# Branch products in pieces of 512 columns: two token blocks against one weight pair

## Chip, cores and metric

The kernel runs on one core of one Trainium2 chip. The metric is the device time of a launch in microseconds: 1518.65 us, the median of three runs (1518.39 to 1519.7).

## What is computed

```python
def _moe2_ref(x, w1, w2, w3, w_out):
    h = np.maximum(np.maximum(x @ w1, x @ w2), x @ w3)
    return (h @ w_out).astype(np.float32)

def reference(**kwargs):
    attn_out = _attn_ref(**attn_kwargs)          # retention, 8 x 8 heads, 576 positions, width 64
    x = attn_out.transpose(0, 2, 1, 3).reshape(4608, 512)
    x = _moe_ref(x=x, **moe_kwargs)              # h = x @ w_in (2048 wide); (h * cos(h)) @ w_out
    return _moe2_ref(x=x, **moe2_kwargs)         # three branches of 512 x 768, their maximum, 768 x 512
```

The change touches the three branch products `x @ w1`, `x @ w2`, `x @ w3` and their maximum, and nothing else of the arithmetic.

## The kernel before

The 4608 tokens are cut into nine blocks of 512 (`NBLK`). The stages follow one another on TensorE: retention with the first half of `w_in`, the second half of `w_in`, `w_out` (tiles `wo`), the three branches (tiles `d_b`, `b_b`, `a_b`), the last product (tiles `o`). Each big matrix product is a Strassen-like scheme: a weight pair (two column tiles of 128 features, four quarters) and a token block in four quarters of 256 columns give seven products, `P_A11` to `P_S4`. Weights and tokens are split into a high and a low part in a reduced fp32 form, so that one product with one pair is six matmuls: low weight by high token and high by high for two halves of the contraction, then high by low twice (`product_in`, L373).

There are nine branch pairs, b0 to b8 (`PAIRS`). All nine stand in SBUF through the branch stage: eight in the eight buffers of `wpool`, b8 in four tiles of `xpool`. `xpool` has 22 buffers of 4 KB a partition, for operands and for results. For every block, `group_in` (L405) takes one or two pairs (`B_GROUPS`: two pairs side by side fill the 512 columns of a PSUM bank, 256 each) and runs the seven products in a fixed order, one per slot. A slot is a call of `tick()`, which runs what was entered in the agenda with `at(n, fn)` for that slot: so the code writes out by hand the order of every engine's instructions. The last product of a group, `P_A22`, is put off to the fifth slot of the next group (`pending`, `last_product`). ScalarE copies three results out of PSUM at L400, L418, L423 and L430, VectorE adds three more at L410, and the maxima run on VectorE at L901 from `branch_half`. A block's seven operands (`build_in`, L661) need four differences, seven copies to the high part on ScalarE (L360) and seven subtractions for the low part on VectorE (L364), 512 columns each; they are made during the block before. The maxima are stored to DRAM tiles `mq` and read back in the last stage by `build_out`. SyncE's queue issues every DMA in the order of the code.

Of the kernel before, what the change touches and what calls it, by code (L numbers as in the profile page):

```python
# [101 lines left out]
def retention_ffn(ctx: ExitStack, tc: tile.TileContext, att, w_in, w_out, w123, w_out2, cst, out):  # L102
# [34 lines left out]
    def at(n, fn):  # L137
        agenda.setdefault(slot[0] + n, []).append(fn)
# [175 lines left out]
        at(6 + more, lambda: st["lows"]())  # L314

    def take(kind, i):
        if (kind, i) == ("b", 8):
            ws = []
            for k in range(4):
                lo, hi = PIECE[k]  # L320
                t = x4(f"w_{kind}{i}_{k}", [hi - lo, 2, HB], F32R)
                nc.sync.dma_start(out=f32(t), in_=stash[kind, i][:, lo:hi])
                ws += [t[:, n] for n in range(hi - lo)]
            weights[kind, i] = ws
            return
# [40 lines left out]
    def load_quarters(o, src):  # L366
        n = o["n"]
        for k in range(2):
            t = o[f"k{k + 1}"] = x4(f"k{k}_{o['name']}", [2, n])
            nc.sync.dma_start(out=t, in_=src[:, 2 * k : 2 * k + 2])  # L370


    def product_in(h, ws, product, x, first):  # L373
        for p, w in enumerate(ws):
# [9 lines left out]
            for i, (a, b) in enumerate(terms):  # L384
# [6 lines left out]
                    skip_group_check=True,  # L391
                )

    pending = []

    def last_product(own_slot=True):

        g = pending.pop()
        product_in(g["d"], g["ws"], P_A22, g["xs"], False)
# [5 lines left out]
    def group_in(ws, xs, name, done, where):  # L405
        n = HB * len(ws)
        g = {"ws": ws, "xs": xs, "name": name, "n": n, "done": done, "at": where}

        def plus(dst, b):
            nc.vector.tensor_tensor(out=dst, in0=dst, in1=b[:, :n], op=ALU.add)  # L410

        def go(b, product, first):
            product_in(b, ws, product, xs, first)

        d = g["d"] = bank(f"d_{name}")
        go(d, P_A11, True)
        s0 = g["s0"] = x4(f"s0_{name}", [2, n])
# [4 lines left out]
        s1 = g["s1"] = x4(f"s1_{name}", [2, n])  # L422
# [454 lines left out]
        )  # L877
    for i in range(len(back) - 3):
        at(28 * i + 5, lambda: background(*back.pop(0), False))
    for k in range(4):  # L880
        for p in range(2):
            at(28 * (NBLK - 1) + 7 * k + 8 + p, lambda k=k, p=p: take("b", 2 * k + p))
    later_y = {}

    def block_in(j, now, k1, k2):
        o = later_y[j] = {"name": f"z{j}", "n": NB}
        at(now, lambda: load_quarters(o, x2q[j]))
# [9 lines left out]
    def store(dst, s):  # L897
        nc.sync.dma_start(out=dst, in_=s)

    def most(dst, a, b):  # L900
        nc.vector.tensor_tensor(out=dst, in0=a, in1=b, op=ALU.max)  # L901

    def branch_half(g, half):
        j, k = g["at"]
        if k in (0, 1) and half:
            best[j, k] = g["s0"]
            at(1, lambda: most(g["s0"], g["s0"], g["s1"]))
        elif k == 2:
            s = g[f"s{half}"]
            at(1, lambda: most(s, s, best.pop((j, half))))  # L910
            at(3, lambda: store(mq[j][0][:, 2 * half : 2 * half + 2], s))
        elif k == 3 and half:
            best[j, k] = g
        elif k == 4 and half:

            def both():
                o = best.pop((j, 3))
                most(g["s0"], g["s0"], g["s1"])
                for p in range(2):
                    s = o[f"s{p}"]  # L920
                    most(s, s, g["s0"][:, :, p * HB : (p + 1) * HB])
                    at(2, lambda p=p, s=s: store(mq[j][1][:, 2 * p : 2 * p + 2], s))

            at(1, both)

    B_GROUPS = [[0, 1], [2, 3], [4, 5], [6], [7, 8]]
    for j in range(NBLK):
        for k, ids in enumerate(B_GROUPS):
            if k == 0 and 1 <= j <= 3:
                background(*back.pop(0), False)  # L930
            if k == 2 and j + 1 < NBLK:
                block_in(j + 1, 4, 9, 13)
            if j == NBLK - 1 and k in (1, 2):
                at(6, lambda k=k: [take("o", i) for i in ((0, 1), (2,))[k - 1]])
            if j == NBLK - 1 and k == 4:
                outs[0, 0] = build_out("m0_0", NB, mq[0][0], range(1, 7), -0)
            group_in([weights["b", i] for i in ids], later_y[j], f"b{j}_{k}", branch_half, (j, k))

    todo = [(j, k) for j in range(NBLK) for k in range(2)]
    outs[0, 1] = build_out("m0_1", HB, mq[0][1], (0, 0, 1, 1, 2, 2), 0)  # L940
    for j in range(1, NBLK):
        at(14 * j - 14, lambda j=j: outs.__setitem__((j, 0), build_out(f"m{j}_0", NB, mq[j][0], (4, 5, 6, 8, 10, 12), 0)))
        at(14 * j - 8, lambda j=j: outs.__setitem__((j, 1), build_out(f"m{j}_1", HB, mq[j][1], (8, 8, 9, 9, 10, 10), 2)))
# [50 lines left out]
```

## Time and profile before

| | us |
|---|---|
| median of three runs | 1518.65 |
| the profiled execution, first to last instruction | 1516.2 |
| the branch stage in it, first to last branch matmul | 958.5 to 1378.6 |
| PE busy, whole span | 1454.9 (96%) |
| PEld (weight loads) busy | 1416.0 (93%) |
| DVE busy | 1224.6 (81%) |
| ACT busy | 726.8 (48%) |
| POOL busy | 268.7 (18%) |

The page shows busy shares by engine; PE is TensorE's matmuls, PEld its weight loads, which run beside the matmuls, DVE is VectorE, ACT ScalarE, POOL GpSimd, SP SyncE. Matmuls overlap in their records, so the number of matmuls that start in a stretch tells more than the length of one. Idle time before an instruction is put down to what ended it (the releaser).

### The profile page before, as it was taken

The page shows a single profiled execution, that of the slowest core. Times are in us where ns is not written, and L with a number is a line of the kernel's source. Part 1 is how long each engine was busy: PE and PEld are TensorE (multiplying, and loading weights), DVE is VectorE, ACT ScalarE, POOL GpSimd, SP SyncE. Part 2 cuts the span into 40 slices and gives each one's busy share as a digit, 9 for nine tenths or more (in the row PEclk, how much of TensorE's full clock was granted, in tenths as well). Part 3 has the DMA queues.
Part 4 walks back from the last instruction along what each step waited for, and adds up shares of the span by engine and source line. Part 5 has one row for each costly group of instructions (what it writes and reads, how often), then busy time and mean ns, then how long its engine had stood idle before and what let it go on. Part 6 is the DMA issues. An engine that isn't in the chain of part 4 may idle for free.

```text
span 1516.2 us, 30767 instructions
## 1 busy us (share of the span) xinstructions
PE 1454.9 (96%) x12506; PEld 1416.0 (93%) x12506; DVE 1224.6 (81%) x1759; ACT 726.8 (48%) x1214; POOL 268.7 (18%) x216
## 2 busy tenths in 40 slices
PE   6899999999899997899999999999999999999998
PEld 5798989998889997899999999999999999999998
DVE  6888999989889989999999998656664555538997
ACT  3555555556667755454445444334432333323332
POOL 3344444444222001100000000000000000004221
PEclk9899999999999998999999999999999999999999
DMA  7588888876989984556555568923431110254443
GB/s 292 181 292 304 309 300 301 318 290 240 355 304 364 328 294 156 184 193 215 193 203 195 196 216 323 397 107 119 147 127 48 70 66 34 70 191 163 168 168 138
DMA packets 83084, 324.46 MB, mean 214 GB/s; under 512 B 9216, under 2 KB 9216, under 8 KB 76928
## 3 DMA queue, kind: packets, MB, share of 16 engines
q1 hardware_dynamic: 82944, 322.51, 59.4%
q8 instruction: 98, 1.61, 0.4%
q14 instruction: 42, 0.34, 0.1%
HBM read 190.35 MB, written 132.12 MB: 213 GB/s over the span
## 4 chain that ended last, share of the span: by engine, by line
PE 46%; DVE 6%; issue 3%; DMA 2%; ACT 1%; POOL 0%; DVEq 0%; SPq 0%; ACTq 0%; POOLq 0%
PE wo L795 17%; PE d_b L385 14%; PE b_b L385 7%; PE o L795 4%; PE a_b L385 3%; DVE l_m L768 1%; DMA st_o<-p_o 1%; DVE tb_m L356 1%; DVE o_o L808 1%; DVE x_m L759 1%; DVE u_o L808 1%; DMA raw_b<-w 1%; DVE l_g L768 0%; DMA k_m<-mq 0%; ACT h_m L763 0%
## 5 line engine op out<-in xcount | busy, mean ns | idle before, releaser
L795 PE MATMUL wo<-h_g,w_wo 128*128 128x256 f32 x1728 | 314.9, 284 | 0.0
L795 PEld LDWEIGHTS wo<-h_g,w_wo 128*128 128x128 f32 x1728 | 271.3, 193 | 0.0
L795 PE MATMUL wo<-l_g,w_wo 128*128 128x256 f32 x864 | 246.6, 285 | 7.6 <-DVE l_g L768 7.6
L385 PE MATMUL d_b<-x_z,w_b 128*128 128x256 f32 x1944 | 248.8, 283 | 2.9 <-ACT s_b L430 2.1
L385 PEld LDWEIGHTS d_b<-x_z,w_b 128*128 128x128 f32 x1944 | 239.9, 192 | 3.7 <-ACT s_b L430 2.7
L795 PEld LDWEIGHTS wo<-l_g,w_wo 128*128 128x128 f32 x864 | 166.7, 193 | 9.6 <-DVE l_g L768 9.5
L385 PE MATMUL b_b<-x_z,w_b 128*128 128x256 f32 x972 | 131.6, 283 | 2.0 <-DVE x_z L364 2.0
L385 PE MATMUL d_a<-x_x,w_wi 128*128 128x256 f32 x864 | 123.2, 293 | 4.1 <-DVE x_x L364 2.9
L385 PEld LDWEIGHTS b_b<-x_z,w_b 128*128 128x128 f32 x972 | 123.2, 192 | 2.2 <-DVE x_z L364 2.2
L385 PE MATMUL d_a<-x_y,w_wi 128*128 128x256 f32 x864 | 115.3, 291 | 9.2 <-ACT s_a L418 5.8
L385 PEld LDWEIGHTS d_a<-x_y,w_wi 128*128 128x128 f32 x864 | 110.9, 199 | 10.4 <-ACT s_a L418 6.5
L385 PEld LDWEIGHTS d_a<-x_x,w_wi 128*128 128x128 f32 x864 | 110.2, 195 | 8.9 <-DVE x_x L364 4.1
L795 PE MATMUL o<-h_m,w_o 128*128 128x256 f32 x648 | 117.5, 283 | 0.0
L763 ACT CAST h_g<-tb_g 128x1024 fp32r<-128x1024 f32 x36 | 37.8, 1051 | 150.5 <-DVE tb_g L356 145.9
L795 PEld LDWEIGHTS o<-h_m,w_o 128*128 128x128 f32 x648 | 101.1, 192 | 0.0
L452 DVE SCALAR_TENSOR_TENSOR t_a<-s_a,t_a 128x1024 f32<-128x1024 f32 x72 | 99.8, 1389 | 1.4 <-ACT t_a L448 1.4
L410 DVE TENSOR_TENSOR s_b<-s_b,b_b 128x512 f32<-128x512 f32 (+1 forms) x45 | 28.5, 634 | 87.1 <-PE b_b L385 87.0
L460 DVE TENSOR_TENSOR s_a<-s_a,t_a 128x1024 f32<-128x1024 f32 x72 | 90.6, 1274 | 5.9 <-ACT t_a L457 5.9
L457 ACT ACTIVATE t_a<-t_a 128x1024 f32<-128x1024 f32 x72 | 76.3, 1062 | 34.8 <-DVE t_a L453 25.6
L410 DVE TENSOR_TENSOR s_b<-s_b,a_b 128x512 f32<-128x512 f32 (+1 forms) x45 | 28.5, 634 | 79.2 <-PE a_b L385 69.4
L795 PE MATMUL o<-l_m,w_o 128*128 128x256 f32 x324 | 91.8, 283 | 0.0
L418 ACT COPY s_b<-d_b 128x512 f32<-128x512 f32 (+1 forms) x45 | 24.5, 544 | 127.3 <-PE d_b L385 120.0
(173 smaller groups left out, 3003.1 us busy)
## 6 DMA issues: line engine op xcount, KB each, us to landing
u<-att SPq DMA_DIRECT2D x36, 1024.0 KB, 7.3
gq<-s_a SPq DMA_DIRECT2D x72, 512.0 KB, 6.4
k_g<-gq SPq DMA_DIRECT2D x72, 512.0 KB, 6.6
xs<-x_x SPq DMA_DIRECT2D x63, 512.0 KB, 7.3
x_y<-xs SPq DMA_DIRECT2D x63, 512.0 KB, 7.9
w_b<-st_b SPq DMA_DIRECT2D x8, 1792.0 KB, 13.0
st_b<-p_b SPq DMA_DIRECT2D x27, 512.0 KB, 3.8
raw_b<-w SPq DMA_DIRECT2D x18, 512.0 KB, 6.1
```

Of the source, the lines that this page charges most:

```text
L356: eng.tensor_tensor(out=d, in0=a, in1=b, op=ALU.subtract)
L385: nc.tensor.matmul(h[:, p * HB : (p + 1) * HB], a, b, start=first and p == 0 and i == 0, stop=i == len(terms) - 1, skip_group_check=True,)
L410: nc.vector.tensor_tensor(out=dst, in0=dst, in1=b[:, :n], op=ALU.add)
L418: nc.scalar.copy(s0[:, 0], d[:, :n])
L452: nc.vector.scalar_tensor_tensor(out=r, in0=s, scalar=INV2PI, in1=st["t"], op0=ALU.mult, op1=ALU.subtract)
L457: nc.scalar.activation(r, r, AF.Sin, scale=TURN, bias=HALF_PI)
L460: nc.vector.tensor_tensor(out=s, in0=s, in1=f32(st["t"]), op=ALU.mult)
L759: nc.vector.tensor_tensor(out=o["x"][:, 1], in0=o["k1"][:, 0], in1=f32(o["x"][:, 0]), op=ALU.subtract)
L763: nc.scalar.copy(h, o[pairs[k][2]])
L768: nc.vector.tensor_tensor(out=lo, in0=o[pairs[k][2]], in1=f32(h), op=ALU.subtract)
L795: nc.tensor.matmul(b[:, mt * HB : (mt + 1) * HB], a, v, start=first and mt == 0 and p == 0 and i == 0, stop=last and p == len(ws) - 1 and ...
L808: nc.vector.scalar_tensor_tensor(out=d, in0=b, scalar=scale, in1=other, op0=ALU.mult, op1=ALU.add)
```

## The change

One block (block 0) stays alone; the other eight make four duos of two blocks (`NDUO`). For a duo, `product_duo` multiplies one weight pair with both blocks: the moving operand is [128, 2 blocks, 256] columns, 512 in one matmul, and fills a PSUM bank. Six matmuls of 512 columns stand where twelve of 256 stood. The nine pairs come in three turns of three groups, one pair in each group: turns 0 and 1 (pairs b0, b2, b4 and b1, b3, b5) run for duo 0, 1, 2, 3; then the pairs b7, b8, b6 are loaded in the place of b0, b2, b4, and turn 2 runs for duo 3, 2, 1, 0. So six pairs stand in SBUF at a time, and the operands of duos 0 to 2 are built twice, those of block 0 too. Two buffers of `wpool` become six places for results (`held`, `give`). `duo_in` writes out the operand build of a duo slot by slot: four loads of 512 KB from `x2p`, four differences, seven high and seven low parts, 1024 elements a partition each; new operands take the buffers of old ones as TensorE leaves them. Both tiles of DRAM (`x2p`, `mqp`) hold two blocks side by side, so that the stores to them go in pieces of 2 KB and 1 KB a partition. The last stage takes the blocks in the order 7, 8, 5, 6, 3, 4, 1, 2, 0.

```diff
+    def product_duo(h, w, product, x, first):
+        wh, wl = w[product][:, 0], w[product][:, 1]
+        xh, xl = x[product]
+        terms = []
+        for kc in range(2):
+            m = slice(kc * 128, kc * 128 + 128)
+            terms += [(wl[:, m], xh[:, :, kc]), (wh[:, m], xh[:, :, kc])]
+        for kc in range(2):
+            m = slice(kc * 128, kc * 128 + 128)
+            terms.append((wh[:, m], xl[:, :, kc]))
+        dst = h.rearrange("p (b n) -> p b n", b=2)
+        for i, (a, b) in enumerate(terms):
+            nc.tensor.matmul(
+                dst, a, b, start=first and i == 0, stop=i == len(terms) - 1, skip_group_check=True
+            )
...
-    for k in range(4):
+    for k in range(3):
         for p in range(2):
             at(28 * (NBLK - 1) + 7 * k + 8 + p, lambda k=k, p=p: take("b", 2 * k + p))
...
-    take("b", 8)
+    free = []
+    for n in range(2):
+        w = w14(f"ext{n}", F32)
+        free += [w[:, 2 * NB * i : 2 * NB * (i + 1)] for i in range(3)]
...
+    def duo_half(g, half):
+        m, turn, k = g["at"]
...
+            def keep():
+                src = s.rearrange("p q (b n) -> p q b n", b=2)
+                for b in range(2):
+                    nc.sync.dma_start(out=to[:, b], in_=src[:, :, b])
+                give(f"s{half}_{name}")
+
+            at(1, finish)
+            at(3, keep)
...
+        steps = (
+            (-14, load, 0),
+            (-13, load, 1),
+            (-13, load, 3),
+            (-12, load, 2),
+            (-8, less, 4, 1, 0),
+            (-7, high, P_A11, 0),
+            (-6, less, 6, 3, 4),
+            (-6, low, P_A11),
+            (-4, less, 5, 3, 1),
+            (-3, high, P_S1, 4),
+            (0, low, P_S1),
+            (1, high, P_A12, 2),
+            (1, less, 7, 6, 2),
...
+            (6, low, P_A22),
+        )
+        for n, fn, *args in steps:
+            at(to + n, lambda fn=fn, args=args: fn(*args))
...
+    DUO_GROUPS = [(0, 2, 4), (1, 3, 5), (7, 8, 6)]
...
+    duo_in(0, "e0", 16)
+    for k in range(3):
+        single_group(k)
+    for m in range(NDUO):
+        if m < 3:
+            at(1, lambda: background(*back.pop(0), False))
+        duo_groups(m, 0)
+        if m + 1 < NDUO:
+            duo_in(m + 1, f"e{m + 1}", 14)
+        else:
+            for n, i in enumerate((7, 8, 6)):
+                at(7 * n - 7 if n else 0, lambda i=i: take("b", i))
+        duo_groups(m, 1)
+    for n, m in enumerate(reversed(range(NDUO))):
...
+            if k == 0:
+                if m:
+                    duo_in(m - 1, f"e{m - 1}b", 14)
+                else:
+                    block_in(0, 2, 10, 13)
+
+        duo_groups(m, 2, begin)
...
+    for k in (3, 4):
...
+        single_group(k)
```

On TensorE, a group before: block 1 with the pairs b2 and b3 (`d`, `b`, `a` are the group's three PSUM banks, `x_z1_…` the operands of block 1).

```order
L385 MATMUL d_b1_1_11698<-x_z1_0_11439,w_b2_10876 128x256 x6
L385 MATMUL d_b1_1_11698<-x_z1_0_11439,w_b3_10894 128x256 x6
L385 MATMUL b_b1_1_11715<-x_z1_3_11462,w_b2_10876 128x256 x6
L385 MATMUL b_b1_1_11715<-x_z1_3_11462,w_b3_10894 128x256 x6
L385 MATMUL a_b1_1_11730<-x_z1_1_11482,w_b2_10876 128x256 x6
L385 MATMUL a_b1_1_11730<-x_z1_1_11482,w_b3_10894 128x256 x6
```

The same three products in the changed kernel: duo 0 with the pair b3 (`h0_e0` and `l0_e0` are the high and low part of the duo's first operand).

```order
L402 MATMUL d_e0_3_11689<-h0_e0_11252,w_b3_10882 128x512 x4
L402 MATMUL d_e0_3_11689<-l0_e0_11269,w_b3_10882 128x512 x2
L402 MATMUL b_e0_3_11701<-h3_e0_11314,w_b3_10882 128x512 x4
L402 MATMUL b_e0_3_11701<-l3_e0_11357,w_b3_10882 128x512 x2
L402 MATMUL a_e0_3_11713<-h1_e0_11372,w_b3_10882 128x512 x4
L402 MATMUL a_e0_3_11713<-l1_e0_11389,w_b3_10882 128x512 x2
```

Each slot has half the matmuls, each twice as wide, and each weight half is loaded for 512 columns.

On VectorE, the change of operands before: the end of block 1, where the operands of block 2 (`z2`) are made between the additions from PSUM (L410) and the maxima (L901).

```order
L410 TENSOR_TENSOR s1_b1_3_11940<-s1_b1_3_11940,d_b1_3_11923 128x256
L356 TENSOR_TENSOR tb_z2_11994<-k1_z2_11890,ta_z2_11951 128x512
L356 TENSOR_TENSOR ta_z2_11951<-k1_z2_11890,k0_z2_11888 128x512
L364 TENSOR_TENSOR x_z2_1_11996<-k1_z2_11890,x_z2_1_11996 128x512
L356 TENSOR_TENSOR tb_z2_11994<-tb_z2_11994,k1_z2_11890 128x512
L410 TENSOR_TENSOR s0_b1_4_12011<-s0_b1_4_12011,a_b1_4_12034 128x512
L364 TENSOR_TENSOR x_z2_4_12032<-tb_z2_11994,x_z2_4_12032 128x512
L364 TENSOR_TENSOR x_z2_6_12049<-k1_z2_11890,x_z2_6_12049 128x512
L364 TENSOR_TENSOR x_z2_5_12065<-ta_z2_11951,x_z2_5_12065 128x512
L410 TENSOR_TENSOR s0_b1_4_12011<-s0_b1_4_12011,b_b1_4_12016 128x512
```

The change of operands from duo 0 to duo 1 in the changed kernel, VectorE again (L423 adds from PSUM, L927 is the maximum, L1008 a difference, L1018 a low part).

```order
L423 TENSOR_TENSOR ext0_11095<-ext0_11095,d_e0_3_11689 128x512
L1018 TENSOR_TENSOR l3_e1_11762<-r4_e1_11687,h3_e1_11737 128x1024
L1008 TENSOR_TENSOR r7_e1_11774<-r6_e1_11709,r2_e1_11656 128x1024
L423 TENSOR_TENSOR ext0_11095<-ext0_11095,a_e0_5_11776 128x512
L1018 TENSOR_TENSOR l1_e1_11784<-r2_e1_11656,h1_e1_11772 128x1024
L1018 TENSOR_TENSOR l4_e1_11795<-r6_e1_11709,h4_e1_11786 128x1024
L1018 TENSOR_TENSOR l6_e1_11806<-r3_e1_11646,h6_e1_11797 128x1024
L423 TENSOR_TENSOR ext0_11095<-ext0_11095,b_e0_5_11764 128x512
L1018 TENSOR_TENSOR l5_e1_11817<-r5_e1_11728,h5_e1_11808 128x1024
L927 TENSOR_TENSOR ext0_11095<-ext0_11095 128x1024
L423 TENSOR_TENSOR ext1_11096<-ext1_11096,d_e0_5_11754 128x512
L1018 TENSOR_TENSOR l2_e1_11829<-r7_e1_11774,h2_e1_11819 128x1024
```

The low parts have twice the columns and stand close together in the last third of a turn, each behind the release of an old operand's buffer.

## Rows read from the trace of the kernel before

**Rows 1.** The page: busy us (share of the span) xinstructions of TensorE and VectorE.

```profile
PE 1454.9 (96%) x12506; PEld 1416.0 (93%) x12506; DVE 1224.6 (81%) x1759; ACT 726.8 (48%) x1214; POOL 268.7 (18%) x216
```

**Rows 2.** Branch stage: length; PE, PEld, DVE, ACT, POOL busy (x started); clock, DMA.

```profile
958.40:1000.00 41.60, 38.80 (x322) 38.40 (x321) 23.78 (x37) 13.01 (x25) 0.00 (x0) 1.00 0.79 308
...
1200.00:1250.00 50.00, 50.00 (x419) 50.00 (x418) 24.46 (x36) 15.94 (x30) 0.00 (x0) 1.00 0.23 74
...
1350.00:1378.60 28.60, 27.05 (x226) 26.85 (x224) 16.77 (x20) 9.30 (x16) 5.79 (x4) 1.00 0.61 213
sum 420.20, PE 415.31 PEld 414.29 DVE 231.51 ACT 143.94 POOL 12.02; mean PE 46.15 PEld 46.03 DVE 25.72 ACT 15.99 POOL 1.34
```

**Rows 3.** Whom TensorE waited for in the branch stage: us, times, longest.

```profile
PE d_b L385 <- ACT s_b L430: 2.1, 3, 1.6
PE b_b L385 <- DVE x_z L364: 2.0, 1, 2.0
PE d_b L385 <- DVE x_z L364: 0.8, 1, 0.8
```

**Rows 4.** Timeline in the branch stage: start, length of the merged row, engine, count.

```profile
1211.17 1.51 PEld L385 LDWEIGHTS a_b<-x_z,w_b 128*128 128x128 f32 x12
1211.29 1.60 PE L385 MATMUL a_b<-x_z,w_b 128*128 128x256 f32 x12
...
1212.61 2.95 PEld L385 LDWEIGHTS d_b<-x_z,w_b 128*128 128x128 f32 x24
1212.73 3.04 PE L385 MATMUL d_b<-x_z,w_b 128*128 128x256 f32 x24
```

**Rows 5.** Matmuls of the branch stage by tile, all of 256 columns (lines view).

```profile
L385 PE MATMUL d_b<-x_z,w_b 128*128 128x256 f32 x1944 | 248.8, 283 | 2.9 <-ACT s_b L430 2.1 <-DVE x_z L364 0.8
...
L385 PE MATMUL b_b<-x_z,w_b 128*128 128x256 f32 x972 | 131.6, 283 | 2.0 <-DVE x_z L364 2.0
...
L385 PE MATMUL a_b<-x_z,w_b 128*128 128x256 f32 x486 | 65.7, 283 | 0.0
```

**Rows 6.** Timeline at half clock, matmuls of 256 columns of the stage `wo`.

```profile
599.32 0.63 PE L795 MATMUL wo<-h_g,w_wo 128*128 128x256 f32 x2
599.75 0.41 PE L795 MATMUL wo<-l_g,w_wo 128*128 128x256 f32 x1
599.96 0.63 PE L795 MATMUL wo<-h_g,w_wo 128*128 128x256 f32 x2
```

**Rows 7.** A stretch at half clock: length, PE busy (x started), granted clock, DMA.

```profile
359.30:362.50 3.20, 3.20 (x15) 0.50 0.59 238
```

**Rows 8.** VectorE and ScalarE by form, 1000 to 1370 us: count, busy, mean ns.

```profile
L901 DVE TENSOR_TENSOR s_b<-s_b,s_b 128x1024 f32<-128x1024 f32 x40 | 48.8, 1221 | 0.0
L410 DVE TENSOR_TENSOR s_b<-s_b,a_b 128x512 f32<-128x512 f32 x33 | 22.7, 688 | 71.9 <-PE a_b L385 65.7 <-ACT p_o L204 5.6
...
L423 ACT COPY s_b<-b_b 128x512 f32<-128x512 f32 x33 | 19.4, 587 | 26.2 <-PE b_b L385 26.2
...
L364 DVE TENSOR_TENSOR x_z<-tb_z,x_z 128x512 fp32r<-128x512 f32 x16 | 11.0, 686 | 0.0
...
L763 ACT CAST h_m<-k_m 128x1024 fp32r<-128x1024 f32 x1 | 1.0, 1045 | 0.5 <-DMA k_m<-mq 0.5
```

**Rows 9.** The dearest low part of 1024 columns, whole span.

```profile
L768 DVE TENSOR_TENSOR l_g<-k_g,h_g 128x1024 fp32r<-128x1024 f32 x36 | 51.5, 1430 | 0.3 <-ACT h_g L763 0.3
```

**Rows 10.** DMA issues: count, KB each, median us from issue to landing.

```profile
w_b<-st_b SPq DMA_DIRECT2D x8, 1792.0 KB, 13.0
...
x2q<-o_wo SPq DMA_DIRECT2D x18, 512.0 KB, 4.0
k_z<-x2q SPq DMA_DIRECT2D x18, 512.0 KB, 5.2
mq<-s_b SPq DMA_DIRECT2D x18, 512.0 KB, 2.6
k_m<-mq SPq DMA_DIRECT2D x18, 512.0 KB, 5.9
```

More of the change, by code (lines that the diff above doesn't have):

```diff
@@ L403, in last_product, with group_in @@
             tick()
[L405 to L407 removed]
+    def group_in(ws, xs, name, done, where, duo=False, tile=None):
+        n = NB if duo else HB * len(ws)
+        g = {"name": name, "n": n, "done": done, "at": where}
+        tile = tile or x4
         def plus(dst, b):
@@ L891, in retention_ffn, with held, give @@
     phase_out("wo", [[2 * k, 2 * k + 1] for k in range(4)], todo, lambda j, k: outs.pop((j, k)), WSCALE**-2, x2q)
-    take("b", 8)
+    free = []
+    for n in range(2):
+        w = w14(f"ext{n}", F32)
+        free += [w[:, 2 * NB * i : 2 * NB * (i + 1)] for i in range(3)]
+    home = {}
+    def held(name, shape):
+        home[name] = t = free.pop(0)
+        return t[:, : shape[0] * shape[1]].rearrange("p (q n) -> p q n", q=shape[0])
+    def give(name):
+        free.append(home.pop(name))
     best = {}
-    def store(dst, s):
-        nc.sync.dma_start(out=dst, in_=s)
     def most(dst, a, b):
@@ L921, in both @@
                     most(s, s, g["s0"][:, :, p * HB : (p + 1) * HB])
-                    at(2, lambda p=p, s=s: store(mq[j][1][:, 2 * p : 2 * p + 2], s))
+                    at(2, lambda p=p, s=s: nc.sync.dma_start(out=mqs[1][:, 2 * p : 2 * p + 2], in_=s))
             at(1, both)
-    B_GROUPS = [[0, 1], [2, 3], [4, 5], [6], [7, 8]]
[L927 to L943, printed above, removed]
+    def duo_half(g, half):
+        m, turn, k = g["at"]
+        name = g["name"]
+        if k < 2 and half:
+            best[k] = g
+            def merge():
+                most(g["s0"], g["s0"], g["s1"])
+                give(f"s1_{name}")
+            at(1, merge)
+        elif k == 2:
+            s, o = g[f"s{half}"], best[half]
+            to = mqp[m][turn // 2][:, :, 2 * half : 2 * half + 2, (turn % 2) * HB : (turn % 2 + 1) * HB]
+            def finish():
+                most(s, s, o["s0"])
+                give(f"s0_{o['name']}")
+            def keep():
+                src = s.rearrange("p q (b n) -> p q b n", b=2)
+                for b in range(2):
+                    nc.sync.dma_start(out=to[:, b], in_=src[:, :, b])
+                give(f"s{half}_{name}")
+            at(1, finish)
+            at(3, keep)
@@ new lines, in retention_ffn, with duo_in, load, less @@
+    duos = {}
+    def duo_in(m, name, to):
+        o = duos[m] = {}
+        r = {}
+        def load(q):
+            t = r[q] = x4(f"r{q}_{name}", [2, 2, HB])
+            nc.sync.dma_start(out=t.rearrange("p b k n -> p b (k n)"), in_=x2p[m][:, q])
+        def less(q, a, b):
+            r[q] = x4(f"r{q}_{name}", [2, 2, HB])
+            nc.vector.tensor_tensor(out=r[q], in0=r[a], in1=r[b], op=ALU.subtract)
+        def high(product, q):
+            h = x4(f"h{product}_{name}", [2, 2, HB], F32R)
+            nc.scalar.copy(h, r[q])
+            o[product] = (h, r[q])
+        def low(product):
+            h, t = o[product]
+            lo = x4(f"l{product}_{name}", [2, 2, HB], F32R)
+            nc.vector.tensor_tensor(out=lo, in0=t, in1=f32(h), op=ALU.subtract)
+            o[product] = (h, lo)
+        steps = (
[12 more added lines that the diff above has]
+            (1, less, 7, 6, 2),
+            (2, low, P_A12),
+            (2, high, P_S2, 6),
+            (3, low, P_S2),
+            (3, high, P_S4, 3),
+            (4, low, P_S4),
+            (4, high, P_S3, 5),
+            (5, low, P_S3),
+            (5, high, P_A22, 7),
+            (6, low, P_A22),
+        )
+        for n, fn, *args in steps:
+            at(to + n, lambda fn=fn, args=args: fn(*args))
@@ new lines, in retention_ffn, with single_group, duo_groups @@
+    B_GROUPS = [[0, 1], [2, 3], [4, 5], [6], [7, 8]]
+    DUO_GROUPS = [(0, 2, 4), (1, 3, 5), (7, 8, 6)]
+    def single_group(k):
+        group_in([weights["b", i] for i in B_GROUPS[k]], later_y[0], f"b0_{k}", branch_half, (0, k), tile=held)
+    def duo_groups(m, turn, begin=None):
+        for k, i in enumerate(DUO_GROUPS[turn]):
+            if begin is not None:
+                begin(k)
+            group_in([weights["b", i]], duos[m], f"e{m}_{i}", duo_half, (m, turn, k), duo=True, tile=held)
@@ new lines, in retention_ffn, with begin @@
+    duo_in(0, "e0", 16)
[12 more added lines that the diff above has]
+    for n, m in enumerate(reversed(range(NDUO))):
+        def begin(k):
+            if k == 0 and n == 1:
+                for i in range(3):
+                    at(2 + 4 * i, lambda i=i: take("o", i))
+            if k == 0:
+                if m:
+                    duo_in(m - 1, f"e{m - 1}b", 14)
+                else:
+                    block_in(0, 2, 10, 13)
+        duo_groups(m, 2, begin)
```

56 lines of the change are left out of this document (35 added, 21 removed).

## The prediction

> **What bounds the kernel now.** I read the page's busy shares first: TensorE is busy 96% of the span and its weight loads 93%, VectorE 81% [rows 1]. A share over the whole span hides the stages, so the branch stage was cut into stretches next. From 1000 us on TensorE has no gap worth a line: 419 matmuls start in 50 us, while VectorE is busy half the time and DMA a fifth [rows 2]. The waits of TensorE in the whole stage are 4.9 us [rows 3], most of it at the stage's start, where 322 matmuls start in 41.6 us instead of some 347. So the stage is one queue of 3402 matmuls (1944 + 972 + 486 [rows 5]) at full clock, and only their spacing matters.
>
> The spacing is to be read from the timeline, since the 283 ns of one record overlap with the next: 24 matmuls of 256 columns take 3.04 us, less the last one's 0.28, by 23 steps: 0.120 us each [rows 4]. 3402 x 0.120 = 408.2 us of the stage's 420.2; the rest are 48 early matmuls of the last product (5.8 us) and some 6 us of stalls.
>
> What makes the 120 ns? At half clock the same matmul, with the same weight load before it, is spaced by 213 ns: three start in the 0.64 us from 599.32 to 599.96 [rows 6], 15 in 3.20 us [rows 7]. Clock 0.50 is the level of 1.2 GHz, and 256 columns at one a tick are 213.3 ns: nothing is left over for the load, which is hidden. At 2.4 GHz 256 columns are 106.7 ns, and the spacing is 120: there 13.3 ns are not columns. The timeline says whose they are: each row of loads starts 0.12 us ahead of its row of matmuls (1211.17 and 1211.29, 1212.61 and 1212.73 [rows 4]), just one spacing, so that a load begins when the matmul before it begins and is ready 0.12 us later. With 256 columns the load is the longer of the two; with 512 columns the matmul is.
>
> **The change part by part.**
>
> *The matmuls.* Block 0 keeps its 378 matmuls of 256 columns (nine pairs x seven products x six). The other eight blocks' 3024 become 1512 of 512 columns. No matmul of 512 columns of this kind is in the trace, so its spacing is bounded: from below by the columns, 512 at 2.4 GHz, as the half-clock rows give them, 0.2133 us; from above by two old spacings, 0.240, if the 120 ns were a rate per column; between them lies 0.2267, if the 13.3 ns were a fixed price of each matmul that adds to its columns. The half-clock rows speak against both of the upper ones: there the extra is nil, as with the longer of two. I take 0.216, close above the columns. The stage then has 378 x 0.120 + 1512 x 0.216 = 45.4 + 326.6 = 372.0 us of matmuls, 36.3 less than 408.2. The ends give 40.3 (0.2133), 20.1 (0.2267) and 0 (0.240).
>
> The Trainium skill, page "TensorE: Matmul & The Clock Gate", section "Back-to-back issue gap", gives an isolated gap of N / 2.4 + 2.5 ns; by it 512 columns would be 215.8 ns and the gain 36.6 us. For 256 columns it gives 109 ns where the trace has 120, so the trace does not agree with it where a weight load goes with each matmul and the columns are few.
>
> *Operands built twice.* Before, nine builds of 512 columns: 11 VectorE instructions of 0.686 us (four differences, seven low parts) and seven ScalarE casts [rows 8]. After: seven duo builds of 1024 columns, and block 0's twice. A VectorE instruction of 1024 columns is 1.22 us (the maximum of that shape; the low part of the last stage is up to 1.43 [rows 9]), a ScalarE cast 1.045 us [rows 8]. A turn is 21 slots of six matmuls, 21 x 6 x 0.216 = 27.2 us. In a turn with a build VectorE has nine additions (0.688), four maxima, four differences and seven low parts: 6.2 + 15 x 1.22 = 24.5 us. ScalarE has twelve copies of 0.587 and seven casts: 14.4 us. Both fit beside TensorE, VectorE with 10% to spare. So the builds cost nothing while that cover holds; with low parts at 1.43 us VectorE would need 26.0 us, still under 27.2. The additions and maxima are as many per block as before, and the waits on them stay.
>
> *The change of operands.* The first new low part (S1) waits until TensorE has done the 15th slot of the old turn, since it takes that buffer; behind it in VectorE's queue stand the rest of the build, three additions and two maxima. Counted from the end of that slot in slots of 1.296 us: S1's low part ends at 1.2 us, the sixth difference at 2.5, an addition at 3.3 (it waits for the 17th slot), three low parts at 4.5, 5.7 and 6.9, an addition at 7.6, then 8.8, a maximum 10.0, an addition 10.7, the last low part 11.9, a maximum 13.2. TensorE wants S1's low part at 9.9 us, the next ones at 11.2, 12.5, 15.1 and 16.4, the last at 22. The margins are 6.7 us or more. The additions run up to 2.3 us late, and TensorE needs the latest of them (the bank `d` of the third group) 2 us after it is done. So no stall at six of the seven changes; at the first, from block 0 to duo 0, the maxima stand in front of the low parts and the margin shrinks to about 1.2 us (S2's low part at 32.4 us, wanted at 33.6 after the stage's start). I put 1 us on the whole for that.
>
> *Queues and DMA.* SyncE's stores of the maxima wait for VectorE, and the loads of the next duo stand behind the first of them; that store can go some 6 us into a turn, the loads land about 5.2 us later [rows 10], and the first difference then ends near 13.2 us of the turn instead of 11.6, which the margins take. A store, now in pieces of 1 KB, must land before ScalarE reuses its place: seven slots, 9.1 us, after its own slot, or some 6 us after a late one, plus 3 us until TensorE wants the bank, against 2.6 us of today's store. The pairs b7, b8, b6 are issued 21 slots or more (27 us) ahead of use, for 13.0 us [rows 10]. The stores of `x2p` in pieces of 2 KB instead of 4 are read a whole turn or more later. Nothing of this is on the path. Three pairs fewer are loaded at the stage's start, where DMA is at 0.79 [rows 2]; I give it no gain, at most the 3 us of stalls there.
>
> *Sum.* The profiled execution's span is 1516.2 us, 2.4 under the median 1518.65, which is time outside the span and stays. 1518.65 - 36.3 + 1.0 = **1483.4 us**; the span would be 1481.
>
> **The rivals.**
>
> *The 13.3 ns stay.* If the change of weights costs a fixed time that only half clock hides, the spacing is 0.2267, the gain 20.1 and the time 1499.5. For it: 120 - 106.7 is a clean rest. Against it: the loads' 0.12 us lead and half clock.
>
> *Nothing gained.* If 2.13 columns per ns were the rate of this moving operand at full clock, the spacing is 0.240 and the time about 1519. Half clock, with one column a tick, speaks against it.
>
> *VectorE becomes the bound.* If its 1024-column instructions are dearer than any row here, or TensorE is held in the order of the queue, then a turn is VectorE's: at 1.43 us for all 15 it is 27.7 us, 0.5 over TensorE in seven turns, 1487. It decides from 1.40 us on; to lose the whole gain, seven turns would have to be 5.2 us longer each.
>
> *The change of operands stalls TensorE.* This is the one on the slow side. If the loads wait for buffers that come free only when the old turn ends, the chain load (5.2), difference (1.2), cast (1.05), low part (1.2) stands in the open at each of seven changes, 8.7 us each, 61 us: 1518.65 - 36.3 + 61 = 1543. It decides from 5.2 us a change. Against it: 22 buffers hold 14 operands of the old duo and eight new tiles, and the four loads come 21 slots ahead.
>
> *Far more gained.* The Trainium skill's page named above, same section, also has a measured sustained spacing of 131 ns at 512 columns with weight loads. By it the time would be 1518.65 - 1512 x 0.109 = 1354. In rows of this kernel the mechanism would be a column in less than a tick, and both 213 ns at half clock [rows 6] and 106.7 of 120 ns at full clock leave no room for it.
>
> **How the numbers follow.** Forecast (spacing 0.213 to 0.218, stalls under 6 us): 0.77. Fixed 13.3 ns: 0.10. VectorE's bound with a few us: 0.05. Nothing gained: 0.04. Stalls at the changes, slower: 0.03. Far more: 0.01. The range reaches from the column bound with the start's stalls gone, 1518.65 - 40.3 - 1 = 1477, to the fixed 13.3 ns, 1500. A measurement of this kernel can tell about 0.2% (3 us) from no change. Faster 0.93, same 0.04, slower 0.03.
>
> **What would show it.** Right: in a timeline of the duo turns six matmuls of 512 columns take 1.30 us from start to start of a slot, some 231 start in 50 us; TensorE's waits in the stage stay under 8 us; VectorE's share there rises from 0.55 to about 0.7; the stage is near 385 us. Wrong: a spacing of 227 or 240 ns; rows of TensorE waiting for the low parts or for ScalarE's copies at the changes; ScalarE waiting for the stores of the maxima.

## The result, and the profile after

The changed kernel takes 1498.91 us, the median of four runs (1497.24 to 1501.92), against 1519.12 us for the kernel before in the same session: a ratio of 0.9863 [0.9847, 0.9879], 20.2 us. The prediction was 1483.4 us, in a range of 1477 to 1500. The time lies inside the range only because its upper end had been put at the price of the rival "the 13.3 ns stay", 1499.5 us, and it is within 1 us of that rival; the forecast itself was 15.5 us too low. The profiled execution has a span of 1498.4 us (its own run 1500.16).

The page's line of busy time, engine by engine, answers to [rows 1]: 1512 matmuls fewer, TensorE as full as before, its loads less, VectorE more.

```profile
PE 1433.9 (96%) x10994; PEld 1335.5 (89%) x10994; DVE 1263.3 (84%) x1739; ACT 745.1 (50%) x1198; POOL 275.4 (18%) x216
```

The branch stage of after by stretches (columns as in [rows 2]: length; busy time of PE, PEld, DVE, ACT, POOL, with the number started; clock, DMA share, GB/s):

```profile
1200.00:1250.00 50.00, 50.00 (x223) 41.40 (x222) 27.88 (x32) 18.56 (x28) 0.00 (x0) 1.00 0.32 111
...
sum 401.10, PE 396.24 PEld 336.60 DVE 270.81 ACT 162.63 POOL 17.84; mean PE 44.03 PEld 37.40 DVE 30.09 ACT 18.07 POOL 1.98
```

In a stretch of duo turns TensorE is never idle and the clock is granted in full, yet 223 matmuls start in 50 us, not 231. VectorE's share of the stage is 270.81 / 401.1 = 0.68, close to the 0.7 forecast. From its first branch matmul to its last the stage runs from 960.9 to 1360.4 us, 399.5 us, against 420.1 before: 20.6 us, which is the whole gain, where some 385 us and so 35 us of gain had been forecast.

Whom TensorE waited for in the stage of after (us, times, longest), to be held against [rows 3]:

```profile
PE d_b L381 <- ACT ext L447: 2.1, 1, 2.1
PE b_b L381 <- DVE x_z L360: 2.0, 1, 2.0
PE d_b L381 <- DVE x_z L360: 0.7, 1, 0.7
```

4.8 us in all, against 4.9 before, and all of it in block 0's groups (tiles `d_b`, `b_b`): 2.7 us at the stage's start and 2.1 us at its end. Before, it was 2.8 us at the start, 1.6 us at the end, where the last block stood then, and 0.5 us between. No duo matmul waits for anything, at none of the seven changes of operands. So what is missing is in the spacing. A timeline of two slots of a duo turn (start, length of the merged row, engine, count):

```profile
1210.53 0.87 PEld L402 LDWEIGHTS d_e<-h_e,w_b 128*128 128x128 f32 x4
1210.75 1.07 PE L402 MATMUL d_e<-h_e,w_b 128*128 128x512 f32 x4
...
1212.11 1.07 PE L402 MATMUL d_e<-h_e,w_b 128*128 128x512 f32 x4
```

From 1210.75 to 1212.11 six matmuls take 1.36 us, 0.2267 us each: the 213.3 ns of their columns and 13.3 ns more. The load rows again lead by one spacing, now 0.22 us. The lines of after by form (1000 to 1340 us; count, busy, mean ns of one) say how long a load is in work, and what the wider instructions of VectorE and ScalarE cost:

```profile
L402 PEld LDWEIGHTS d_e<-h_e,w_b 128*128 128x128 f32 x424 | 79.6, 188 | 16.5
...
L927 DVE TENSOR_TENSOR ext<-ext,ext 128x1024 f32<-128x1024 f32 x31 | 38.8, 1252 | 0.0
...
L1018 DVE TENSOR_TENSOR l_e<-r_e,h_e 128x1024 fp32r<-128x1024 f32 x22 | 26.3, 1219 | 0.0
...
L1012 ACT CAST h_e<-r_e 128x1024 fp32r<-128x1024 f32 x21 | 21.5, 1054 | 0.0
...
L440 ACT COPY ext<-b_e 128x512 f32<-128x512 f32 x35 | 20.6, 588 | 24.0 <-PE b_e L402 20.3 <-DMA mqp<-ext 2.4 <-DVE ext L927 1.3
```

By these records a load of 188 ns that begins one spacing (227 ns) ahead of its matmul is done some 35 to 40 ns before it. The end of the load does not set this spacing, and the matmul still does not follow at its columns' pace.

The page's DMA issues of the stage (count, KB each, median us to landing), against [rows 10]:

```profile
mqp<-ext SPq DMA_DIRECT2D x48, 256.0 KB, 3.2
...
r_e<-x2p SPq DMA_DIRECT2D x16, 512.0 KB, 6.5
```

### The profile page after: what moved, and what is told of

The parts are those of the page before. It is cut to its first block, busy times and chain, and to the rows that moved or that the text cites. A ratio compares the mean times of both kernels' runs of the same rounds, so it can differ in the third digit from the quotient of the medians.

```text
span 1498.4 us, 27726 instructions
## 1 busy us (share of the span) xinstructions
PE 1433.9 (96%) x10994; PEld 1335.5 (89%) x10994; DVE 1263.3 (84%) x1739; ACT 745.1 (50%) x1198; POOL 275.4 (18%) x216
## 4 chain that ended last, share of the span: by engine, by line
PE 46%; DVE 5%; DMA 3%; issue 3%; ACT 1%; SPq 1%; POOL 0%; DVEq 0%; POOLq 0%; ACTq 0%
PE d_e L402 13%; PE wo L812 12%; PE o L812 9%; PE b_e L402 7%; PE a_e L402 3%; DMA raw_b<-w 2%; DMA k_g<-gq 1%; PE d_b L381 1%; DVE l_g L785 1%; PE b_b L381 1%; DVE o_wo L825 1%; DVE tb_g L352 1%; DVE p_b L221 0%; DVE ta_g L352 0%; DMA k_m_first<-mqp 0%
## 5 line engine op out<-in xcount | busy, mean ns | idle before, releaser
L402 PE MATMUL d_e<-h_e,w_b 128*128 128x512 f32 x432 | 115.5, 389 | 0.0
L812 PE MATMUL o<-h_m,w_o 128*128 128x256 f32 x576 | 104.4, 283 | 0.0
L402 PEld LDWEIGHTS d_e<-h_e,w_b 128*128 128x128 f32 x432 | 81.0, 188 | 16.7
L812 PEld LDWEIGHTS o<-h_m,w_o 128*128 128x128 f32 x576 | 89.8, 192 | 0.0
L812 PE MATMUL o<-l_m,w_o 128*128 128x256 f32 x288 | 81.7, 284 | 0.0
L188 POOL TENSOR_TENSOR fa_b<-raw_b 128x512 uint32<-128x512 uint32 x18 | 23.4, 1302 | 313.4 <-DVE raw_b L182 232.2
L548 ACT COPY u<-state 128x128 f32<-128x128 f32 x128 | 32.5, 266 | 93.4 <-PE state L564 93.2
L465 ACT ACTIVATE t_a<-s_a 128x1024 int32<-128x1024 f32 x72 | 75.9, 1057 | 1.5 <-DVE s_a L423 0.7
L423 DVE TENSOR_TENSOR ext<-ext,b_e 128x512 f32<-128x512 f32 x36 | 24.7, 686 | 61.2 <-PE b_e L402 61.2
L564 PE MATMUL state<-u 128*128 128x128 f32 (+1 forms) x256 | 56.4, 309 | 14.4 <-ACT u L548 10.4
```

The source lines that it names most:

```text
L188: eng.tensor_tensor(out=dst.bitcast(U32), in0=r[:, :, 0], in1=r[:, :, 1], op=ALU.add)
L402: nc.tensor.matmul(dst, a, b, start=first and i == 0, stop=i == len(terms) - 1, skip_group_check=True)
L465: nc.scalar.activation(st["t"], s, AF.Copy, scale=INV2PI, bias=0.25)
L548: nc.scalar.copy(um, st)
L564: nc.tensor.matmul(state[:, hp * CH : (hp + 1) * CH], kn[p : p + m, sl], v[p : p + m, sl], start=False, stop=True, skip_group_check=True,)
L812: nc.tensor.matmul(b[:, mt * HB : (mt + 1) * HB], a, v, start=first and mt == 0 and p == 0 and i == 0, stop=last and p == len(ws) - 1 and ...
```

## The experiments

**Streams of one shape each.** A program of nothing but matmul streams, 48 or 96 to a stream, each matmul with its weight load, for the spacing by itself.

```diff
+    stream("one", 512, 48)
+    stream("two", 512, 48, moving=x[:, :, 0])
+    stream("alt", 512, 48, banks=2)
+    stream("same", 512, 48, same=True)
+    stream("few", 512, 48, m=64)
...
+    stream("bfa", 512, 48, moving=xb[:, :512], weights=wb)
```

> Computes nothing of the reference: it runs only streams of matmuls in the reduced fp32 form, each with its own weight load, 48 or 96 in a row into one PSUM bank (name of the bank: stream), then three streams after a pause of 30 us, then ends. Its time means nothing, only the spacing of starts in each stream does. Theory 1, a sum: at full clock the spacing is columns / 2.4 GHz + 13.3 ns whatever the columns: 512 (one, two, same) 226.7, 384 (colsa) 173.3, 320 (colsb) 146.7, 256 (colsc) 120, 192 (colsd) 93, 128 (colse) 67 unless a floor of the load stands above it. Theory 2, the longer of load and columns, and the 13.3 ns of the changed kernel come from its moving operand's two pieces: one 213 to 216, two 227, 384 160, 320 133, 256 to 128 all 120. Theory 3, the price is the weight load's, by its columns: few and fewer (64 columns of weights) at 220 and 113, by theory 1 227 and 120. Theory 4, the price is that of a bank written twice in a row: alt (two banks in turn) 213 to 216, by theory 1 227. Half clock: 512 and 256 columns 427 and 213 (no extra, as in the kernel before); 128 columns 107 by the columns alone, or about 165 if the load is the longer.

The timeline of TensorE in this program, one row a stream (start, length, tile, shape of the weights, shape moved). The spacing is the difference of two rows' starts by the first one's count:

```profile
21.24 11.04 PE L146 MATMUL one<-x,w 128*128 128x512 f32 x48
32.12 11.04 PE L146 MATMUL two<-x,w 128*128 128x512 f32 x48
43.00 11.04 PE L146 MATMUL alt<-x,w 128*128 128x512 f32 x48
53.88 11.04 PE L146 MATMUL same<-x,w 128*128 128x512 f32 x48
64.76 11.20 PE L146 MATMUL few<-x,w 128*64 128x512 f32 x48
75.80 8.51 PE L146 MATMUL colsa<-x,w 128*128 128x384 f32 x48
84.14 7.19 PE L146 MATMUL colsb<-x,w 128*128 128x320 f32 x48
91.17 11.67 PE L146 MATMUL colsc<-x,w 128*128 128x256 f32 x96
102.69 11.05 PE L146 MATMUL fewer<-x,w 128*64 128x256 f32 x96
113.58 10.86 PE L146 MATMUL colsd<-x,w 128*128 128x192 f32 x96
124.28 10.85 PE L146 MATMUL colse<-x,w 128*128 128x128 f32 x96
134.97 10.53 PE L146 MATMUL bfa<-xb,wb 128*128 128x512 bf16 x47
145.34 10.64 PE L146 MATMUL bfb<-xb,wb 128*128 128x256 bf16 x96
```

(32.12 - 21.24) / 48 = 0.2267 us: the kernel's spacing, with nothing else going on. It is the same for one piece of 512 columns (`one`), for two blocks side by side (`two`), for two PSUM banks in turn (`alt`) and for one weight tile loaded again and again (`same`). 320 columns give 0.1465, 256 give 0.1200: with the columns' 133.3 and 106.7 taken off, 13 ns remain at each width, so that this is a price of the matmul (with its load) and not a rate per column. That is the first of the four theories; the longer of load and columns, and the bank written twice in a row, are out. A load of 64 columns changes the spacing, but not one way: 0.230 at 512 columns (`few`), 0.1134 at 256 (`fewer`). 192 and 128 columns both give 0.111, so that a load of 128 columns, whatever it takes, lets a matmul follow every 0.111 us, below the 0.120 of the kernel before. Two-byte operands (`bfa`) give (145.34 - 134.97) / 48 = 0.216 at 512 columns, 2.7 ns above them.

Of the streams after a pause, the one of 128 columns ran at half clock at first (columns of the row as in [rows 2]):

```profile
240.03:243.00 2.97, 2.97 (x14) 2.97 (x15) 0.00 (x0) 0.00 (x0) 0.00 (x0) 0.50 0.00 0
```

14 matmuls of 128 columns start in 2.97 us, 0.21 us each, no faster than those of 256 columns in [rows 7]. So at half clock, too, there is a floor under the spacing, and 256 columns stand just on it.

**The same stage with halves.** Everything of the change stays (duos, turns, builds, DMA), but a slot issues twelve matmuls of 256 columns again.

```diff
-        dst = h.rearrange("p (b n) -> p b n", b=2)
-        for i, (a, b) in enumerate(terms):
-            nc.tensor.matmul(dst, a, b, ...)
+        for n in range(2):
+            for i, (a, b) in enumerate(terms):
+                nc.tensor.matmul(h[:, n * HB : (n + 1) * HB], a, b[:, n], ...)
```

> The changed kernel, but each duo product as twelve matmuls of 256 columns again (block by block) in place of six of 512. Everything else, the turns, the builds made twice, the DMAs, stays. Theory 1 (13.3 ns for each matmul, and nothing else gains or costs): 1512 x 13.3 ns = 20.1 us more than the changed kernel's 1498.9, so 1519, ratio 1.000 to the kernel before. Rival: part of the gain came from elsewhere (fewer loads at the stage's start, other order): 1505 to 1515. Rival: the second builds cost something that the wide matmuls pay back: over 1523.

1520.6 us, ratio 0.9999 [0.9987, 1.001]. One stretch of its stage (columns PE, PEld, DVE, ACT):

```profile
1200.00:1250.00 50.00, 50.00 (x419) 50.00 (x418) 20.71 (x25) 12.60 (x21) 1.00 0.45 158
```

419 matmuls in 50 us, as in [rows 2], and the time that the first theory gave. The width of the matmul, with one weight load for 512 columns in place of two, is the whole of the gain; the new order of work by itself costs and brings nothing, within 0.13%.

**Operands built once.** Turn 2 runs on duo 3's operands throughout, so that three second builds with their loads are gone.

```diff
                 if m:
-                    duo_in(m - 1, f"e{m - 1}b", 14)
+                    duos[m - 1] = duos[m]
```

> The changed kernel, but turn 2 uses the operands of duo 3 for all four duos (so the outputs are not the reference's): the three second builds of duos 2, 1, 0, with 33 instructions on VectorE (40 us), 21 casts on ScalarE (22 us) and 12 loads of 512 KB, are gone. Theory: all of it lay beside matmuls, so 1498.9 within 1.5 us, ratio 0.986. Rival: the second build costs TensorE waits at each change of operands: 3 us or more faster, ratio 0.984 or less.

1501.85 us, ratio 0.9873 [0.9854, 0.9892] in its session, against 0.9863 [0.9847, 0.9879] with the builds. One stretch of this kernel (columns as in [rows 2]):

```profile
955.00:1340.00 385.00, 382.29 (x1827) 322.88 (x1827) 222.46 (x281) 138.62 (x225) 8.53 (x6) 1.00 0.36 126
```

and the same stretch of after:

```profile
955.00:1340.00 385.00, 382.22 (x1839) 322.79 (x1838) 262.19 (x317) 158.87 (x249) 8.53 (x6) 1.00 0.41 145
```

VectorE has 40 us less to do, ScalarE 20 us less, and TensorE is busy for the same 382 us. The second builds are hidden.

**All low parts twice.** How much more VectorE work does the stage take? Each of the 49 low parts of the duo builds is issued a second time, 60 us in all.

```diff
-            nc.vector.tensor_tensor(out=lo, in0=t, in1=f32(h), op=ALU.subtract)
+            for _ in range(2):
+                nc.vector.tensor_tensor(out=lo, in0=t, in1=f32(h), op=ALU.subtract)
```

> The changed kernel, but each low part of a duo's operands is computed twice (49 more VectorE instructions of 1.22 us, 60 us in all). In a turn with a build VectorE then has 6.2 + 22 x 1.22 = 33.0 us, where TensorE's 126 matmuls at 226.7 ns take 28.6. Theory (VectorE is covered, with margins of 7 us at a change): turns 0 and 1 of the first pass catch up in the light turns and cost nothing; the three builds in a row of the second pass run up 3 x 4.4 = 13 us, 7 of it under cover: 4 to 9 us slower than 1498.9, so 1503 to 1508. Rival (no cover, VectorE is already on the path): up to 60 us more, over 1520. Rival (VectorE has more slack than counted): 1499.

1540.0 us, ratio 1.013 [1.0109, 1.0152]: 41 us more than after, far more than the 4 to 9 us that I expected, and inside what the rival "no cover" allowed. TensorE's waits in its stage (us, times, longest):

```profile
PE d_e L402 <- DVE ext L423: 20.8, 9, 5.9
...
PE b_e L402 <- ACT ext L440: 1.9, 1, 1.9
PE d_e L402 <- DVE l_e L1019: 1.7, 2, 0.9
```

The new operands (L1019 here) are late by 0.9 us at most. What is late is the addition from the bank `d` (L423): it stands behind the low parts in VectorE's queue, and TensorE may not write the bank again until it is done. I had taken the margin of the operands, about 7 us, for the margin of the whole queue. How small the margin of that addition is can be read in after itself. At the change from duo 2 to duo 1 it ends at 1282.90 us, and TensorE writes the bank again (the group's last product, still on the operands `h_e2b`) at 1284.24:

```profile
1282.22 0.68 DVE L423 TENSOR_TENSOR ext<-ext,d_e 128x512 f32<-128x512 f32 x1
...
1284.24 1.07 PE L402 MATMUL d_e<-h_e2b,w_b 128*128 128x512 f32 x4
```

That is 1.3 us in hand; at the other five changes from duo to duo the same two records lie 2.5 to 3.0 us apart. Five low parts stand ahead of this addition, so doubling them puts 6.1 us more in front of it. Then the clock (stretches of this kernel, columns as in [rows 2]):

```profile
1250.00:1300.00 50.00, 45.27 (x198) 36.48 (x197) 45.05 (x46) 19.00 (x28) 0.00 (x0) 1.00 0.45 167
1300.00:1350.00 50.00, 39.92 (x164) 31.98 (x165) 43.98 (x43) 20.57 (x29) 0.00 (x0) 0.94 0.26 81
1350.00:1410.00 60.00, 57.69 (x357) 52.74 (x357) 42.67 (x54) 20.96 (x37) 9.29 (x6) 0.94 0.33 109
```

TensorE stood still for 4.7 and 10 us in the first two of these stretches, and part of the time from 1300 us on was granted at the lower level. Over the stage the parts below 1.00 come to about 11 us of full clock, where after had 1.00 in every stretch; with 26.7 us of waits in the duo turns that is 38 of the 41 us. VectorE was not full even here, 45.05 of 50 us at most, so that the order of its queue counts and not its load alone.

**Two low parts twice.** To try that corrected reading: only the first two low parts of a change (S1 and A12) twice, 17 us of VectorE, 2.4 us more ahead of the addition from bank `d`.

```diff
+            for _ in range(2 if product in (P_S1, P_A12) else 1):
```

> The changed kernel, but only the first two low parts (S1, A12) of each duo's operands are computed twice: 14 more VectorE instructions of 1.22 us, 17 us in all, 2.4 us in each of the seven builds. The run with all low parts doubled was 41 us slower, with TensorE waiting for additions from the bank d. Theory: what VectorE has in hand at a change of operands is the time to the addition from the third group's bank d: at slots of 1.36 us that addition ends 10.9 us after the end of the 15th slot and TensorE wants the bank at 13.6, so 2.7 us. With 2.4 us more in front of it TensorE still does not wait: within 2 us of the changed kernel's 1498.5, ratio 0.986 to 0.9875. Rival: VectorE is on the path already, each added us counts as in the run before (41 of 60 us): 11 to 12 us slower, 1510, ratio 0.9935.

1503.47 us, ratio 0.9883 [0.9858, 0.9907]. TensorE's waits in its duo turns:

```profile
PE d_e L402 <- DVE ext L423: 1.1, 1, 1.1
PE d_e L402 <- ACT ext L447: 0.7, 1, 0.7
PE b_e L402 <- ACT ext L440: 0.4, 1, 0.4
```

Between the two expectations, nearer to the first, though TensorE does wait: one addition is late, by 1.1 us, at the last change (from duo 1 to duo 0, 2.5 us in hand in after). At the change before it, with only 1.3 us in hand in after, two copies of ScalarE had held TensorE for 0.4 and 0.7 us, and the addition was done 0.2 us in time. The 0.9935 of the other reading lies outside the interval; the ratio is not told apart from the 0.986 [0.9847, 0.9874] of the changed kernel measured once more beside the next two kernels (1498.46 us):

> The changed kernel itself, beside the two versions that follow: 1498.9 us, ratio 0.986 to the kernel before.

**The stall at the stage's end.** In after the last group's copy from the bank `d_b` comes late. Timeline of after (in brackets: idle before, and what ended it):

```profile
1348.92 0.62 ACT L772 CAST x_m_first<-k_m_first 128x512 fp32r<-128x512 f32 x1 [3.64 <-DMA k_m_first<-mqp]
...
1351.13 0.58 ACT L447 COPY ext<-d_b 128x512 f32<-128x512 f32 x1
...
1351.77 1.70 PE L381 MATMUL d_b<-x_z,w_b 128*128 128x256 f32 x12 [2.08 <-ACT ext L447]
```

ScalarE's queue holds a cast of the next stage that waits 3.64 us for its load; the copy (L447) stands behind it, and TensorE behind the copy. The kernel before had the same stall there, 1.55 us. The build of that operand was entered one group earlier, with the loads ahead of it:

```diff
     for k in (3, 4):
-        if k == 4:
-            outs[ORDER[0], 0] = build_out("m_first", NB, mq[ORDER[0]][0], range(1, 7), -0)
+        if k == 3:
+            outs[ORDER[0], 0] = build_out("m_first", NB, mq[ORDER[0]][0], range(5, 11), -0)
```

> The changed kernel, but the operands of the first block of the last stage are loaded one group (seven slots) earlier and built three slots earlier. Theory: the one wait of TensorE at the end of the branch stage (2.1 us on a copy of ScalarE, which stood behind a cast that waited for that load) goes: 2 us faster than the changed kernel, 0.1%, at the edge of what five rounds tell. Rival: VectorE and ScalarE, busy with the last operands there, push another wait in its place: no change.

1495.95 us, ratio 0.9833 [0.9815, 0.9851]: 2.5 us less than after beside it, about what the wait was, though the intervals overlap, so that the times alone do not show it. Its waits in the stage, with that of L447 gone:

```profile
PE b_b L381 <- DVE x_z L360: 2.0, 1, 2.0
PE d_b L381 <- DVE x_z L360: 0.8, 1, 0.8
```

**And the stall at the stage's start.** On top of the edit before, the preparation of the pair b8, which runs on VectorE among the operands of block 0, moves from the last block of the stage `wo` to the first duo turn. The three preparations of the last product's pairs go one duo turn later each; the fourth of these turns had none.

```diff
-    for i in range(len(back) - 3):
+    for i in range(len(back) - 4):
...
-        if m < 3:
-            at(1, lambda: background(*back.pop(0), False))
+        at(1, lambda: background(*back.pop(0), False))
```

> As the run before, and in addition the splitting of the pair b8, which the changed order needs only in its last turn, moves from the last block of the stage wo to the first duo turn, and those of the last product's three pairs one duo turn later each (the fourth of these turns had none). Theory: the 2.7 us for which TensorE waits for the first operands at the stage's start come from VectorE's queue, in which the parts of b8 stand between them; they go, and the sum of both is 4 to 5 us faster than the changed kernel, about 1494, ratio 0.983. Rival: VectorE is full there with the stage wo's own work, and only 1 us comes.

1493.87 us (1492.36 to 1496.49), ratio 0.983 [0.9816, 0.9845]. Its interval lies just clear of that of after beside it: 4.6 us faster than the changed kernel, 26 us than the one before, and the fastest kernel here. The 2.7 us at the stage's start have become 0.5, and a new wait of 1.2 us has come in a duo turn. What TensorE still waits for in its stage:

```profile
PE b_e L402 <- ACT ext L440: 1.2, 1, 1.2
PE b_b L381 <- DVE x_z L360: 0.5, 1, 0.5
```

**Is it the load's width?** In the first program a load of 64 columns of weights had changed the spacing at 256 columns (`fewer`), so widths of 128, 96, 64 and 32 were run against 512, 384 and 256 columns moved.

```diff
+    for name, n, m in (
+        ("a", 512, 128), ("b", 512, 96), ("c", 512, 64), ("d", 512, 32),
+        ("e", 384, 128), ("f", 384, 96), ("g", 384, 64), ("h", 384, 32),
+        ("i", 256, 128), ("j", 256, 96), ("k", 256, 64), ("l", 256, 32),
+    ):
+        stream("s" + name, n, 48, m=m)
```

> Computes nothing of the reference: streams of 48 matmuls as before, now with weights of 128, 96, 64 and 32 columns (streams sa to sd at 512 moving columns, se to sh at 384, si to sl at 256), two-byte operands (bfa: 512 by 128; bfb: 512 by 64; bfc: 256 by 64), and at the end short streams after a pause. Theory: the price above the columns at full clock is the four-byte load's and goes with its columns: at 256 moving columns 120.0, 116.7, 113.3, 110.0; at 384 173.3, 170.0, 166.7, 163.3; at 512 226.7, 223.3, 220.0, 216.7, as far as these are above the floor of about 110 that loads alone have. Rival: it is a price per matmul, and the 113 of 64 columns at 256 was something else: then 173.3 and 226.7 for all. Two-byte operands: 215.8 and 109 whatever the load. Half clock: 427, 320, 213 for 512, 384, 256 columns, nothing above the columns.

Timeline rows of TensorE, spacing as above:

```profile
21.02 11.04 PE L146 MATMUL sa<-x,w 128*128 128x512 f32 x48
31.91 11.21 PE L146 MATMUL sb<-x,w 128*96 128x512 f32 x48
42.95 11.20 PE L146 MATMUL sc<-x,w 128*64 128x512 f32 x48
...
98.50 5.91 PE L146 MATMUL si<-x,w 128*128 128x256 f32 x48
104.25 5.73 PE L146 MATMUL sj<-x,w 128*96 128x256 f32 x48
109.82 5.61 PE L146 MATMUL sk<-x,w 128*64 128x256 f32 x48
115.27 5.60 PE L146 MATMUL sl<-x,w 128*32 128x256 f32 x48
```

At 512 columns a narrower load saves nothing: 0.2269 with 128 columns of weights, (42.95 - 31.91) / 48 = 0.230 with 96. At 256 columns it saves half of the 13.3 ns (0.1198, 0.1160, 0.1135 with 128, 96, 64 columns of weights), and 32 columns save no more. Neither expectation held whole. At half clock the extra is not there (stretch of the same program, eight matmuls of 384 columns in 2.56 us, 0.320 each, just their columns at 1.2 GHz):

```profile
182.34:184.90 2.56, 2.56 (x8) 2.56 (x9) 0.00 (x0) 0.00 (x0) 0.00 (x0) 0.50 0.00 0
```

So the load's width is not the cause at 512 columns, the changed kernel's shape; at 256, the shape of before, half of the 13.3 ns goes with it. What takes the 13.3 ns at 2.4 GHz with four-byte operands, in the matmul or in the fact that a load goes with it, stays open.

## Why the prediction was right and wrong

**The spacing: the step that failed.** The term "1512 x 0.216 = 326.6" is 1512 x 0.2267 = 342.7 us, 16.2 more; with it, and without the 1 us for stalls that were not there, the prediction's own sum gives 1483.4 + 16.2 - 1.0 = 1498.6 us, and 1498.91 was measured. The mechanism of the forecast, that the 13.3 ns are time of the load which 512 columns hide, did not hold; the time lies in the range because the rival's price was its end. Two readings led there. The first: "a load begins when the matmul before it begins and is ready 0.12 us later". The rows show only when the load begins, not that the matmul waits for its end. [rows 4] spoke against it already: 12 loads fill 1.51 us, which leaves 1.51 - 11 x 0.12 = 0.19 us for the record of one, more than its lead of 0.12. In after the lead is again one spacing, 0.22 us, with a load of 188 ns, and streams with the same loads go down to 0.111 us, under the 0.120 of the kernel before. So with 256 columns the 0.120 us were not the time of a load, though half of the 13.3 ns does go with its width there. The second: "nothing is left over" at half clock was carried to full clock. At half clock the extra is nil for matmuls that at full clock have it (384 columns: 0.320, and 0.174 at 2.4 GHz against 0.160 of columns), and the 0.213 of 256 columns is also what 128 columns take there, so that it was as much a floor as the columns. That row could not speak for the longer of two against a price of each matmul, and the price was given 0.10 where the other had 0.77.

**The rival that happened.** "The 13.3 ns stay" had the size right (gain 20.1 against 20.2 us). Its owner, a cost of changing weights, is not shown: the stream that loads one tile again and again has the same spacing at 512 columns, and those with narrower loads have no less, so that neither new weights nor the load's width makes the price there. Whether it would go with no load at all wasn't tried.

**What the trace could have told.** 0.120 us less 106.7 ns was a clean rest, and no row of the branch stage had another width to hold against it. The formula of the Trainium skill, page "TensorE: Matmul & The Clock Gate", section "Back-to-back issue gap", N / 2.4 + 2.5 ns, holds here for two-byte operands (215.8 ns by it, 0.216 measured) and not for the four-byte form of this kernel (226.7); I had put its failure at 256 columns down to few columns. The same section's 131 ns at 512 columns was seen in no stream here.

**Nothing gained, far more gained.** Both fell: 0.2267 is neither 0.240 nor 0.131.

**Builds twice at no cost.** Right: three second builds fewer bring no time. The low parts are 1.22 us, the casts 1.054, as taken; the maxima are 1.252, not 1.22.

**VectorE and the changes of operands.** Right that neither binds: no duo matmul waits. But the margins of "6.7 us or more" are the operands'. The narrow place is the one that the prediction names last, the bank `d`, put at 2 us and measured at 1.3 to 3.0: 2.4 us more in front of it made one addition late, by 1.1 us, 6.1 us more made the kernel 41 us slower. The rival's "It decides from 1.40 us on" was a sum over the turn, where the queue's order within it decides: with two low parts doubled the sum of a turn, 6.2 + 17 x 1.22 = 26.9 us, is still under TensorE's 28.6, and TensorE waited.

**The stage's start.** 1 us was put on the first change; nothing was lost there, and stalls of the old size stayed (4.9 and 4.8 us). Most of them could be had: the kernel with both moves is 4.6 us faster.

**Queues and DMA.** Right for TensorE. The loads of the duos took 6.5 us in the first pass instead of 5.2, and ScalarE waited once, 2.4 us, for a store of the maxima (the row of L440): that sign of the list under "Wrong" did appear, and TensorE's distance from the copy took it up.

## What to carry to other kernels

Read a matmul's price from full-clock rows of two widths. If there is only one, don't count on a wider matmul to cover the rest above the columns: here it was a price of each matmul, and a row at half clock couldn't decide that. Wider matmuls with the same work then gain that price once for each matmul saved, here 1512 x 13.3 ns = 20.1 us. When an engine gets more work beside the path, look in its queue for the instruction with the shortest time to its reader, which may be an old one that stands behind the new.

## What the runs showed of the hardware

- With four-byte operands (fp32r) at 2.4 GHz a matmul with a load of 128 weight columns costs its columns and 13 ns, at 512, 384, 320 and 256 columns; with two-byte operands its columns and 2.7 ns (512 columns in 0.216 us). At 1.2 GHz four-byte operands cost nothing above the columns (384 columns in 0.320 us).
- With four-byte operands and 128 columns of weights a stream doesn't go below 0.111 us a matmul at full clock, whether 192 or 128 columns move, and at half clock not below 0.21 us, whether 256 or 128 move.
- A narrower weight tile makes the matmul of 256 columns cheaper, 0.1198 to 0.1135 us, and that of 512 columns dearer, 0.2269 to 0.230.
- Waits of TensorE can cost more than their length: in the kernel with all low parts doubled 26.7 us of waits in the duo turns went with about 11 us lost to the lower clock, a stretch's mean down to 0.94. Not each did: with 4.7 us of standing still in 50 one stretch kept 1.00.
